# Two interleaved recurrent layers on one core: the last two segments projected in one pass, one-layer steps reordered, the down projection in column pairs, idle transposes ahead of the last block

## The chip, the cores and the metric

One core of one Trainium2 chip. The metric is device microseconds of one execution; the kernel before took 1579.52 us, the median of three runs (1578.43 to 1586.14).

## The reference

The program runs the same pair twice over 2048 tokens of width 448: a recurrent attention (A), then a gated feed-forward block (B), each behind a layer norm and with a residual.

```
x = x + A(layernorm(x));  x = x + B(layernorm(x))
x = x + A(layernorm(x));  x = x + B(layernorm(x))

A: mem = mem0                                  # 8 rows
   for each of 64 segments of 32 tokens:
       h = concat(mem, segment)                # 40 rows
       q, k, v = h Wq, h Wk, h Wv              # 16 heads of 256
       p = softmax(mask(q k^T / 16))           # causal; the memory rows see all rows
       o = (p v) Wo
       mem, out = o[:8], o[8:]
B: up = x W_up;  gate = x W_gate;  out = (relu(gate) * up) W_down     # width 1792
```

The memory rows make the segments of one layer follow one another. Inputs, weights and output are bfloat16.

## The kernel before, in words

**Setup.** Wq and Wk are fused into A_sb (and A3, A3z for the last 64 dimensions), Wv and Wo into B_sb, so that one segment needs: projection of h by A_sb (`prj`), scores with h itself (`Sm` for the 8 memory rows, `Sx` for the 32 segment rows), softmax (`weights_begin`, `weights_end`), weighting of h by the probabilities (`weigh_m`, `weigh_x`, tiles `ya`, `yb`, `ym`, `y1`, `y2`), and projection by B_sb (`project_out`, tile `ox`, 168 matmuls, and `project_tail`, tile `o3`, 56 matmuls in two column halves of the array for the last 64 dimensions).

**Steps.** The two layers run interleaved: step g works on segment g of the first layer (chain 0) and on segment g-4 of the second (chain 1, LAG = 4). So steps 0 to 3 have chain 0 alone, steps 4 to 63 both, steps 64 to 67 chain 1 alone. The output of a segment's tokens is projected one step later than its memory rows: step g weighs the tokens of its segment at the end (`weigh_x` writes YY[hf] of the next step) and step g+1 projects them together with its own memory rows. The columns that a projection reads run from `lo` to `hi`: 80 where both chains are there, 40 or 32 in one-layer steps. Step 68 has no chain and only projects the tokens of segment 67. YY holds Y0, Z0 (first half of the heads) and Y1, Z1 (second), taken in turn by the parity of the step.

**Feed.** Two segments of 32 make a block of 64 tokens. `Feed(i)` does for block i of the first layer (partitions 64 to 127 of its tiles) and block i-2 of the second (partitions 0 to 63) what follows attention: residual add (`residual`, which flips OT by TensorE, tile `otp`), layer norm (`norm`, and `row_stats` on DVE and POOL), the flip of tokens to columns (`xposed`: four transposes `tps`, then xT is copied by DVE and ACT), `gate_up` in seven parts (tiles `ups`, `gps`, 28 matmuls each, two row halves of the array), `down` (tile `dps`, 14 matmuls of 448 columns), the norm for the next layer (`norm2`), `feed_on` and `leave`, which writes the output. Odd steps from 3 on carry Feed((g-3)/2), cut into the step's matmuls; Feed(33) follows step 68. Feeds 0 and 1 have only a first-layer block, 32 and 33 only a second-layer block: there `self.n` is 64 of the 128 columns.

**Order.** TensorE's matmuls keep the written order (`in_order` chains them). DVE, ACT and POOL run their own queues in an order that a scheduler sets. PSUM tiles named "ps" come from one pool of seven banks, taken in turn.

In one-layer steps the written order behind the scores was: Sx of the first half, the Feed's flip of tokens, Sm and Sx of the second half, the flip of PM0 (`pps`), `weigh_m`, then `project_out`. POOL fills the tiles TZ0 and TZ1 with pieces of the identity before the first step (L405).

Of the kernel before, what the change touches and what calls it, by code (L numbers as in the profile page):

```python
# [8 lines left out]
BF = mybir.dt.bfloat16  # L9
# [44 lines left out]
def build_kernel(ctx, tc, A_x, A_mem0, A_Wq, A_Wk, A_Wv, A_Wo, B_W_gate, B_W_up, B_W_down, out,  # L54
# [29 lines left out]
    def tr(*a):  # L84
        in_order(nc.tensor.transpose(*a))  # L85
# [125 lines left out]
        nc.vector.tensor_copy(mem_cols(g, cs)[:, 0:n], src)  # L211


    with tc.tile_pool(name="pre", bufs=3) as pre:
        mem0_n = pre.tile([MEM, 512], BF, name="mem0_n", bufs=1)
        nc.gpsimd.dma_start(mem0_n[:, 0:DM], mem0)
# [110 lines left out]
            load_next()  # L327
            return transposed(nat[i], i == 0)

        warm = psum.tile([P, 2 * DM], BF, tag="ps", name="warm")  # L330
        def idle(n):
            for _ in range(n):
                tr(warm[:, 0:128], ident[:], ident[:])

        idle(32)
        cur = flip_next(0)
        idle(16)
# [70 lines left out]
    nc.vector.memset(OT[:], 0.0)  # L408
    xT = main.tile([P, NPASS, 128], BF, name="xT")
    hh = main.tile([P, FT, 128], BF, name="hh")  # L410
    nc.gpsimd.memset(hh[:], 0.0)
    HK = []
    for i in range(2):
# [5 lines left out]
    class Feed:  # L419


        def __init__(self, i):
            self.i = i
            self.first = i < nblk
            self.second = 0 <= i - LAG // BLK < nblk
            self.n = slice(0 if self.second else TB, P if self.first else TB)
            self.x = xa[i % 3]
            self.nx = xp[i % 2]

        def residual(self):  # L430
            tp = flipped_dims("otp", lambda r, kd: OT[ROWS[r], kd, :])
# [7 lines left out]

        def xposed(self):  # L440
            tps = transpose_tokens(self.xn)
            nc.vector.tensor_copy(xT[:, 0:4, :], tps[:])
            for r in range(2):
                nc.scalar.copy(xT[ROWS[r], 4:NPASS, :], tps[ROWS[1 - r], 0:3, :])  # L444

        def gate_up(self, u):
            n = self.n
# [12 lines left out]

        def down(self):
            i = self.i
            dps = self.dps = psum.tile([P, 512], F32, tag="ps", name="dps")
            for f in range(FT):
                mm(dps[:, 0:DM], hh[:, f, :], Wd_sb[:, f, :], start=(f == 0), stop=(f == FT - 1))
            if self.first:
                nc.vector.tensor_tensor(self.nx[TB:P, :], dps[TB:P, 0:DM], self.x[TB:P, :], op=ALU.add)
# [11 lines left out]
        def leave(self):  # L479
            i = self.i  # L480
            if self.second:
                nc.vector.tensor_tensor(self.x[0:TB, :], self.dps[0:TB, 0:DM], self.x[0:TB, :], op=ALU.add)
                nc.sync.dma_start(out_dram[block(i - LAG // BLK)], self.x[0:TB, :])

        def feed_on(self):
# [103 lines left out]
        nc.vector.tensor_copy(PT[:], pps[:].rearrange("p b q -> p (b q)"))  # L589
        return PT  # L590

    def flipped_rows(srcs):
# [7 lines left out]
        PT = main.tile([P, n * 128], BF, tag=f"PTr{n}", name="PT")  # L600
# [9 lines left out]
    def step(g, ff):  # L610
# [4 lines left out]
        hb = hTb[gb % 2]  # L615
        cols = [(0, 32) if c == 0 else (48, 80) for c in xs] + [(32, 40) if c == 0 else (40, 48) for c in ms]
        lo, hi = min(a for a, _ in cols), max(b for _, b in cols)
        ox = None

        def ys(hf, later=0):  # L620
# [62 lines left out]

        def weigh_x(hf, hk, PT):

            def keep(eng, c, t0, src):
                n = src.shape[-1] // SEG
                dst = ys(hf, 1)[:, t0:t0 + n, XO[c]:XO[c] + SEG]
# [12 lines left out]
            for kd in (2, 3):  # L701
                for c in chains:
                    rows = slice(64 * c, 64 * c + L)
                    mm(y2[c][:, kd * 256 - 512:kd * 256 - 256], hk[rows, kd, :], PT[rows, 0:256], start=True, stop=True)
            for c in chains:
                keep(nc.scalar if c == 0 else nc.vector, c, 16, y2[c][:, 0:256])
                tail = y2[c][:, 256:512].rearrange("p (o e i q) -> p e i o q", o=2, e=2, i=4)
                for e in range(2):
                    rows = slice(64 * e, 64 * e + 64)
                    evac(nc.vector if c == 0 else nc.scalar,  # L710
                         ys(hf, 1)[rows, 24:28, XO[c]:XO[c] + SEG].rearrange("p i (o q) -> p i o q", q=16),
                         tail[rows, e])

        def project_out(hf, t0, t1):

            nonlocal ox
            if ox is None:
                ox = psum.tile([P, 3, W], F32, tag="ox", bufs=1, name="ox")
            for t in range(t0, t1):
                for mc in range(3):  # L720
                    mm(ox[:, mc, lo:hi], B_sb[:, hf, t, mc * 128:(mc + 1) * 128],
                       ys(hf)[:, t, lo:hi], start=(hf == 0 and t == 0 and mc == 0),
                       stop=(hf == 1 and t == NT - 1 and mc == 2), skip_group_check=True)

        def project_tail():

            o3 = psum.tile([P, W], F32, tag="ps", name="o3")
            for hf in range(2):
                for t in range(0, NT, 2):
                    for e in range(2):  # L730
                        mm(o3[64 * e:64 * e + 64, lo:hi], B_sb[:, hf, t + e, 384:DM], ys(hf)[:, t + e, lo:hi],
                           start=(hf == 0 and t == 0), stop=(hf == 1 and t == NT - 2))
# [6 lines left out]
            for c in xs:  # L739
                x = slice(XO[c], XO[c] + SEG)  # L740
                nc.vector.tensor_tensor(ot_cols(c)[:, 3], o3[:, x], swap[:, x], op=ALU.add)

        def ot_cols(c):
            o = (g - 1) % BLK * SEG + (TB if c == 0 else 0)
# [2 lines left out]
        def finish():  # L747
            if ms:
                src = ox[:, :, M0:M0 + 16].rearrange("p k (c m) -> p k c m", m=MEM)
                set_mem(g + 1, src[:, :, ms[0]:ms[-1] + 1, :], ms, 3)  # L750
            for c in xs:
                nc.scalar.copy(ot_cols(c)[:, 0:3], ox[:, :, XO[c]:XO[c] + SEG])

        def feed(*us):
            if ff is not None:
# [34 lines left out]
        close_bank(c0, chains, hb, j, nc.scalar)  # L790
        close_bank(c2, chains, hb, j, nc.scalar)
        close_bank(c1, chains, hb, j, nc.vector)
        close_bank(c3, chains, hb, j, nc.scalar)
        if len(chains) == 2:
            pm = flipped(PM[0], 1, "m0")
            Sx0 = scores_x(0)
            weigh_m(0, hk, pm)
            if ff is not None:
                ff.xposed()
            scores_m(1)  # L800
            Sx1 = scores_x(1)
            probs_x(0, Sx0)
        else:
            Sx0 = scores_x(0)
            if ff is not None:
                ff.xposed()
# [122 lines left out]
```

## Time and profile before

| what | value |
|---|---|
| three runs | 1578.43, 1579.52, 1586.14 us |
| the profiled execution | 1585.95 us, span 1584.0 us |
| mean granted TensorE clock | 0.990 |
| PE busy | 1552.8 us, 98% of the span, 45116 matmuls |
| DVE, ACT, POOL busy | 1112.6, 783.1, 174.9 us |

A row of a group gives the line, the engine, the operation, what it writes and reads, its shape and count, then busy time in us, the mean duration of one in ns, and the engine's idle time just before, with what ended it. A row of the timeline starts with the start and the length in us; in brackets stands the idle time before it and its releaser. PEld is the loading of weights, which runs beside the matmuls; a matmul's duration holds a pipeline tail of some 0.16 us that the next one covers. "issue" means that the engine waited for nothing that the profile shows.

### The profile page before, as it was taken

Reading aid. Unit: us, or ns where it says so; the run is one execution under the profiler, and the core shown is the slowest. Engines: PE = TensorE matmul, PEld = TensorE weight load, DVE = VectorE, ACT = ScalarE, POOL = GpSimd, SP = SyncE. Lnnn points to the kernel's source line nnn. Section 1 sums busy time; section 2 is a strip of 40 time slices with the busy share of each in tenths; the row PEclk is TensorE's granted clock in tenths of the full one; section 3 lists DMA queues with packets and bytes.
Section 4 is the critical chain, followed back from the end, with each engine's and each line's share of the span. In section 5 each row is a group of like instructions: output and inputs, shape, how many; then the busy total and the mean of one; then the engine's idle time right before and its main releaser. Section 6 shows DMA issues by size and latency. Waiting matters only on the chain.

```text
span 1584.0 us, 98180 instructions
## 1 busy us (share of the span) xinstructions
PE 1552.8 (98%) x45116; PEld 1426.0 (90%) x45116; DVE 1112.6 (70%) x3825; ACT 783.1 (49%) x2307; POOL 174.9 (11%) x308
## 2 busy tenths in 40 slices
PE   9889999999999999999999999999999999999997
PEld 7588899999999999999999999999999999999885
DVE  6755677776777777776777677777767777777663
ACT  6634445544455545554455545544445545544442
POOL 3201110111011111111011111011001111011110
PEclk9989999999999999999999999999999999999998
DMA  9530000000000000000000000000000000000000
GB/s 284 148 80 8 9 10 5 9 10 10 10 10 10 10 10 6 8 10 10 10 10 10 10 10 7 7 10 10 10 10 10 10 10 8 6 8 7 7 7 6
DMA packets 29469, 33.13 MB, mean 21 GB/s; under 512 B 3320, under 2 KB 28160, under 8 KB 29056
## 3 DMA queue, kind: packets, MB, share of 16 engines
q1 hardware_dynamic: 28848, 26.74, 6.2%
q8 instruction: 353, 5.78, 1.5%
q14 instruction: 60, 0.49, 0.1%
q10 hardware_dynamic: 144, 0.11, 0.1%
q0 software_dynamic: 64, 0.01, 0.0%
HBM read 23.18 MB, written 1.84 MB: 16 GB/s over the span
## 4 chain that ended last, share of the span: by engine, by line
PE 95%; DVE 2%; issue 1%; ACT 1%; DMA 1%; POOL 1%; SPq 0%; POOLq 0%; ACTq 0%; DVEq 0%
PE prj L82 30%; PE ox L82 25%; PE ups L82 10%; PE dps L82 6%; PE o L82 5%; PE y L82 4%; PE Sx L82 3%; PE Sm L82 2%; PE aps L82 1%; PE pps L85 1%; PE gps L82 1%; PE bps L82 1%; PE tps L85 1%; PE kps L85 1%; PE ym L82 1%
## 5 line engine op out<-in xcount | busy, mean ns | idle before, releaser
L82 PEld LDWEIGHTS <-B_sb 128*128 128x128 bf16 (+1 forms) x15456 | 495.1, 103 | 29.6 <-issue 21.6
L82 PE MATMUL prj<-hT,A_sb 128*128 128x80 bf16 (+1 forms) x11424 | 430.7, 200 | 0.1
L82 PEld LDWEIGHTS <-A_sb 128*128 128x128 bf16 x11424 | 406.3, 100 | 8.5 <-issue 0.2
L82 PE MATMUL ox<-Y,B_sb 128*128 128x80 bf16 (+4 forms) x5880 | 223.1, 199 | 1.9 <-DVE Y L661 1.9
L94 ACT CAST TQ<-prj 128x480 bf16<-128x480 f32 (+1 forms) x380 | 183.1, 494 | 83.7 <-PE prj L82 59.2
L82 PE MATMUL ox<-Z,B_sb 128*128 128x80 bf16 (+2 forms) x5712 | 217.6, 199 | 1.3 <-DVE Z L661 1.3
L82 PE MATMUL ups<-xT,Wgu_sb 64*128 64x128 bf16 (+1 forms) x3332 | 191.3, 214 | 1.3 <-DVE hh L458 0.8
L82 PE MATMUL gps<-xT,Wgu_sb 64*128 64x128 bf16 (+1 forms) x3332 | 191.3, 214 | 0.4 <-ACT xT L444 0.3
L82 PEld LDWEIGHTS <-Wgu_sb 64*128 64x128 bf16 x6664 | 179.7, 95 | 4.4 <-issue 2.3
L96 DVE CAST TQ<-prj 128x480 bf16<-128x480 f32 (+1 forms) x228 | 129.5, 574 | 17.3 <-PE prj L82 11.7
L458 DVE SCALAR_TENSOR_TENSOR hh<-gps,ut 128x256 bf16<-128x256 f32 (+1 forms) x238 | 94.5, 407 | 48.2 <-ACT ut L457 35.4
L457 ACT CAST ut<-ups 128x256 bf16<-128x256 f32 (+1 forms) x238 | 85.5, 359 | 82.7 <-PE gps L82 64.1
L94 ACT CAST Y<-y 64x128 bf16<-64x128 f32 (+2 forms) x256 | 89.4, 379 | 46.5 <-DVE Y L96 41.5
L96 DVE CAST Y<-y 64x128 bf16<-64x128 f32 (+2 forms) x256 | 102.2, 420 | 14.2 <-ACT Y L94 4.3
L94 ACT COPY hT<-tps 128x256 bf16<-128x256 bf16 x32 | 11.9, 372 | 199.0 <-DVE hT L96 199.0
L96 DVE CAST Z<-y 64x128 bf16<-64x128 f32 (+2 forms) x256 | 99.2, 418 | 12.4 <-ACT Z L94 5.5
L589 DVE COPY PT<-pps 128x128 bf16<-128x128 bf16 (+1 forms) x206 | 49.9, 256 | 80.5 <-PE pps L85 77.7
L94 ACT CAST Z<-y 64x128 bf16<-64x128 f32 (+2 forms) x256 | 89.2, 378 | 23.8 <-DVE Z L96 17.4
L82 PE MATMUL dps<-Wd_sb,hh 128*128 128x448 bf16 x476 | 99.3, 362 | 0.0
L94 ACT CAST TZ<-prj 64x320 bf16<-64x320 f32 (+2 forms) x152 | 56.1, 380 | 86.4 <-DVE TZ L96 78.5
L577 DVE TENSOR_REDUCE ssum<-se 128x2 f32<-128x80 f32 (+1 forms) x270 | 70.8, 274 | 35.8 <-ACT se L571 33.6
L82 PE MATMUL prj<-hT,A 64*128 64x80 bf16 (+1 forms) x3264 | 93.9, 196 | 1.8 <-issue 1.4
(130 smaller groups left out, 2265.7 us busy)
## 6 DMA issues: line engine op xcount, KB each, us to landing
wo<-in_A_Wo_dram SPq DMA_DIRECT2D x8, 448.0 KB, 5.1
nat<-in_A_Wq_dram SPq DMA_DIRECT2D x8, 384.0 KB, 6.1
nat<-in_A_Wk_dram SPq DMA_DIRECT2D x8, 384.0 KB, 6.2
nat<-in_A_Wv_dram SPq DMA_DIRECT2D x8, 384.0 KB, 6.1
xa<-in_A_x_dram SPq DMA_DIRECT2D x32, 56.0 KB, 2.3
xa<-xp SPq DMA_DIRECT2D x32, 56.0 KB, 1.9
out_dram<-xa SPq DMA_DIRECT2D x32, 56.0 KB, 2.0
xp<-in_A_x_dram SPq DMA_DIRECT2D x30, 56.0 KB, 2.1
```

Of the source, the lines that this page charges most:

```text
L82: in_order(nc.tensor.matmul(*a, **k))
L85: in_order(nc.tensor.transpose(*a))
L94: nc.scalar.copy(dst, src)
L96: eng.tensor_copy(dst, src)
L457: nc.scalar.copy(ut[:, :, n], ups[:, :, n])
L458: nc.vector.scalar_tensor_tensor(out=hh[:, 2 * u:2 * u + 2, n], in0=gps[:, :, n], scalar=0.0, in1=ut[:, :, n], op0=ALU.max, op1=ALU.mult)
L577: nc.vector.tensor_reduce(ssum[:], se[:], axis=AX.X, op=ALU.add)
L589: nc.vector.tensor_copy(PT[:], pps[:].rearrange("p b q -> p (b q)"))
```

## The change

1. **Segments 66 and 67 of the second layer are projected together.** Step 66 writes the tokens' weighted rows 32 columns further left, step 67 writes its own beside them in the same tiles, projects nothing and ends behind `down` and `leave`; step 68 projects 64 columns at once and hands OT both segments.
2. **One-layer steps:** the flip of PM0 stands right behind Sx of the first half, and `weigh_m` before Sx of the second half. The Feed's flip of tokens stands between the last two projections; its norm runs on DVE in place of POOL.
3. **One-sided Feeds (0, 1, 32, 33):** `down` takes 64 columns of hh as weights and alternates between the two column halves of the array and two PSUM banks; `sum_up` adds the two parts and the residual (one ACT copy and two DVE adds in place of one DVE add). xT is copied for the 64 columns in use.
4. **Idle transposes:** 44 behind the last Feed's residual and 8 behind its flip, which is done twice so that DVE and ACT copy from tiles of their own. The helper `idle` is defined further up and takes a tile of 128 columns at each call.

```diff
+    def idle(n):
+        warm = psum.tile([P, 128], BF, tag="ps", name="warm")
+        for _ in range(n):
+            tr(warm[:], ident[:], ident[:])
...
         def xposed(self):
             tps = transpose_tokens(self.xn)
-            nc.vector.tensor_copy(xT[:, 0:4, :], tps[:])
+            nc.vector.tensor_copy(xT[:, 0:4, self.n], tps[:, :, self.n])
+            return tps
+
+        def xposed_rest(self, tps):
             for r in range(2):
-                nc.scalar.copy(xT[ROWS[r], 4:NPASS, :], tps[ROWS[1 - r], 0:3, :])
+                nc.scalar.copy(xT[ROWS[r], 4:NPASS, self.n], tps[ROWS[1 - r], 0:3, self.n])
...
         def down(self):
-            dps = self.dps = psum.tile([P, 512], F32, tag="ps", name="dps")
+            dps = self.dps = [psum.tile([P, 512], F32, tag="ps", name="dps") for _ in range(1 if self.both else 2)]
             for f in range(FT):
-                mm(dps[:, 0:DM], hh[:, f, :], Wd_sb[:, f, :], start=(f == 0), stop=(f == FT - 1))
+                if self.both:
+                    mm(dps[0][:, 0:DM], hh[:, f, :], Wd_sb[:, f, :], start=(f == 0), stop=(f == FT - 1))
+                else:
+                    mm(dps[f % 2][ROWS[f % 2], 0:DM], hh[:, f, self.n], Wd_sb[:, f, :], start=(f < 2), stop=(f >= FT - 2))
...
+        def sum_up(self, dst, o):
+            n = slice(o, o + TB)
+            if self.both:
+                nc.vector.tensor_tensor(dst[n, :], self.dps[0][n, 0:DM], self.x[n, :], op=ALU.add)
+                return
+            mine = o // TB
+            nc.scalar.copy(part[n, 1, :], self.dps[1 - mine][ROWS[1 - mine], 0:DM])
+            nc.vector.tensor_tensor(part[n, 0, :], self.dps[mine][n, 0:DM], self.x[n, :], op=ALU.add)
+            nc.vector.tensor_tensor(dst[n, :], part[n, 0, :], part[n, 1, :], op=ALU.add)
...
+        last = g == nseg + LAG - 1
+        now = 0 if chains else 1
+        if not chains:
+            lo -= SEG
...
+            kept = ys(hf, 0 if last else 1)
+            xo = (None, XO[1] - SEG) if g == nseg + LAG - 2 else XO
...
-            ff.norm(nc.gpsimd)
+            ff.norm(nc.gpsimd if len(chains) == 2 else None)
...
         close_bank(c1, chains, hb, j, nc.vector)
+        if ff is not None and len(chains) == 1:
+            tps = ff.xposed()
         close_bank(c3, chains, hb, j, nc.scalar)
+        if ff is not None and len(chains) == 1:
+            ff.xposed_rest(tps)
...
         else:
             Sx0 = scores_x(0)
-            if ff is not None:
-                ff.xposed()
+            pm = flipped(PM[0], 1, "m0") if ms else None
             scores_m(1)
+            weigh_m(0, hk, pm)
             Sx1 = scores_x(1)
-            pm = flipped(PM[0], 1, "m0")
-            weigh_m(0, hk, pm)
             probs_x(0, Sx0)
+        if last:
+            probs_x(1, Sx1)
+            feed(0, 1, 2, 3)
+            px0 = flipped_rows([(PX[0], 2)])
+            feed(4)
+            weigh_x(0, hk, px0)
+            feed(5)
+            px1 = flipped_rows([(PX[1], 2)], "x1")
+            feed(6)
+            weigh_x(1, hk, px1)
+            ff.down()
+            ff.leave()
+            return
...
     ff.residual()
+    idle(44)
     ff.norm()
     ff.xposed()
+    ff.xposed_rest(transpose_tokens(ff.xn))
+    idle(8)
     for u in range(FT // 2):
         ff.gate_up(u)
```

More of the change, by code (lines that the diff above doesn't have):

```diff
@@ L328, in flip_next @@
             return transposed(nat[i], i == 0)
[L330 to L333, printed above, removed]
         idle(32)
@@ L410, in build_kernel @@
     hh = main.tile([P, FT, 128], BF, name="hh")
+    part = main.tile([P, 2, DM], F32, name="part")
     nc.gpsimd.memset(hh[:], 0.0)
@@ L428, in __init__ @@
             self.nx = xp[i % 2]
+            self.both = self.first and self.second
         def residual(self):
@@ L481, in leave @@
             if self.second:
-                nc.vector.tensor_tensor(self.x[0:TB, :], self.dps[0:TB, 0:DM], self.x[0:TB, :], op=ALU.add)
+                self.sum_up(self.x, 0)
                 nc.sync.dma_start(out_dram[block(i - LAG // BLK)], self.x[0:TB, :])
@@ L599, in flipped_rows @@
                 tr(two[r][:, b, :], src[ROWS[r]], ident[ROWS[r], ROWS[r]])
-        PT = main.tile([P, n * 128], BF, tag=f"PTr{n}", name="PT")
+        PT = main.tile([P, n * 128], BF, tag=f"PTr{n}{tag}", name="PT")
         for r, eng in enumerate((nc.vector, nc.scalar)):
@@ L617, in step, with outs @@
         lo, hi = min(a for a, _ in cols), max(b for _, b in cols)
+        last = g == nseg + LAG - 1
+        now = 0 if chains else 1
+        if not chains:
+            lo -= SEG
+        def outs():
+            if not chains:
+                return [(slice(lo, lo + TB), OT[:, :, 0:TB])]
+            return [(slice(XO[c], XO[c] + SEG), ot_cols(c)) for c in xs]
         ox = None
@@ L721, in project_out @@
                     mm(ox[:, mc, lo:hi], B_sb[:, hf, t, mc * 128:(mc + 1) * 128],
-                       ys(hf)[:, t, lo:hi], start=(hf == 0 and t == 0 and mc == 0),
+                       ys(hf, now)[:, t, lo:hi], start=(hf == 0 and t == 0 and mc == 0),
                        stop=(hf == 1 and t == NT - 1 and mc == 2), skip_group_check=True)
@@ L730, in project_tail @@
                     for e in range(2):
-                        mm(o3[64 * e:64 * e + 64, lo:hi], B_sb[:, hf, t + e, 384:DM], ys(hf)[:, t + e, lo:hi],
+                        mm(o3[64 * e:64 * e + 64, lo:hi], B_sb[:, hf, t + e, 384:DM], ys(hf, now)[:, t + e, lo:hi],
                            start=(hf == 0 and t == 0), stop=(hf == 1 and t == NT - 2))
@@ L738, in project_tail @@
                                         swap[:, both].rearrange("p (c m) -> p c m", m=MEM), op=ALU.add)
-            for c in xs:
-                x = slice(XO[c], XO[c] + SEG)
-                nc.vector.tensor_tensor(ot_cols(c)[:, 3], o3[:, x], swap[:, x], op=ALU.add)
+            for x, ot in outs():
+                nc.vector.tensor_tensor(ot[:, 3], o3[:, x], swap[:, x], op=ALU.add)
         def ot_cols(c):
@@ L750, in finish @@
                 set_mem(g + 1, src[:, :, ms[0]:ms[-1] + 1, :], ms, 3)
-            for c in xs:
-                nc.scalar.copy(ot_cols(c)[:, 0:3], ox[:, :, XO[c]:XO[c] + SEG])
+            for x, ot in outs():
+                nc.scalar.copy(ot[:, 0:3], ox[:, :, x])
         def feed(*us):
@@ L798, in step @@
             if ff is not None:
-                ff.xposed()
+                ff.xposed_rest(ff.xposed())
             scores_m(1)
```

9 lines of the change are left out of this document (4 added, 5 removed).

## The prediction

> **What bounds the kernel now.** I read the page first: slices, engine shares, chain, costliest groups.
>
> ```profile
> PEclk9989999999999999999999999999999999999998
> PE 95%; DVE 2%; issue 1%; ACT 1%; DMA 1%; POOL 1%; SPq 0%; POOLq 0%; ACTq 0%; DVEq 0%
> L82 PEld LDWEIGHTS <-B_sb 128*128 128x128 bf16 (+1 forms) x15456 | 495.1, 103 | 29.6 <-issue 21.6
> ```
>
> TensorE carries 95% of the chain that ended last, and the clock (one digit for each fortieth of the span) is below full only in an early slice and in the last. The change leaves the order of every engine in the two-layer steps 6 to 63 alone, so some 1,300 us of the span should stay as they are. What it touches are the one-layer steps 0 to 3 and 64 to 67, step 5's Feed, the drain (step 68) and the last Feed. So the windows of the end come next; columns: stretch, its length, then busy time of PE, PEld, DVE, ACT, POOL with counts, granted clock, DMA share, GB/s.
>
> ```profile
> 1549.50:1552.91 3.41, 2.20 (x71) 1.59 (x64) 1.53 (x5) 1.15 (x6) 0.00 (x0) 1.00 0.02 5
> 1552.91:1556.33 3.42, 3.42 (x12) 1.37 (x10) 0.17 (x1) 0.00 (x0) 0.00 (x0) 0.50 0.00 0
> ...
> 1566.57:1569.98 3.41, 0.91 (x33) 0.69 (x29) 1.26 (x4) 0.24 (x1) 0.63 (x2) 1.00 0.00 0
> 1569.98:1573.39 3.41, 1.95 (x46) 1.64 (x48) 1.03 (x3) 1.08 (x3) 0.17 (x1) 0.50 0.00 0
> 1573.39:1576.81 3.42, 3.42 (x138) 3.42 (x133) 1.44 (x5) 1.19 (x5) 0.00 (x0) 0.50 0.02 5
> ```
>
> A thinly filled stretch of 3.41 us at clock 1.00 (PE busy 2.20, then 0.91) is followed each time by one or more at 0.50. Idle TensorE is thus paid twice, and the last Feed runs mostly at half clock. Then the timeline and the groups by form of steps 67, 68 and the last Feed:
>
> ```profile
> 1543.14 0.23 PE L82 MATMUL Sx<-maskS,ident 128*128 128x160 bf16 x1
> 1551.46 0.97 PE L82 MATMUL o<-Z,B_sb 128*64 128x32 bf16 x50 [1.21 <-issue]
> L82 PE MATMUL dps<-Wd_sb,hh 128*128 128x448 bf16 x14 | 4.5, 503 | 0.0
> L82 PE MATMUL ox<-Y,B_sb 128*128 128x32 bf16 x168 | 4.6, 185 | 0.0
> 1567.52 0.29 PE L85 MATMUL otp<-ident,OT 64*128 64x64 bf16 x8 [0.33 <-ACT OT L752]
> 1570.64 0.61 PE L85 MATMUL tps<-ident,xn 128*128 128x128 bf16 x4 [2.83 <-DVE xn L187]
> 1571.74 0.97 ACT L444 COPY xT<-tps 64x384 bf16<-64x384 bf16 x2 [4.28 <-DVE xT L442]
> L82 PE MATMUL ups<-xT,Wgu_sb 64*128 64x64 bf16 x98 | 5.3, 230 | 0.5 <-DVE xT L442 0.5
> 1580.15 0.62 DVE L482 TENSOR_TENSOR xa<-dps,xa 64x448 bf16<-64x448 f32 x1 [2.18 <-PE dps L82]
> ```
>
> Sx0 of step 67 starts at 1543.14, the drain's output is flipped at 1567.52, 24.4 us later; the last matmul ends near 1580.15 and one DVE add and the output's DMA follow. All of this is serial. The sum below goes part by part over this profiled execution: 1585.95 us, of which 1584.0 are the span and 1.95 lie around it.
>
> **Steps 67 and 68 as one projection.** Removed from step 67: 168 ox and 56 o matmuls, the swap copies and adds behind them, and a flip whose result nobody read. Step 68 does the same counts once, 64 columns wide. What 64 columns cost is not in the trace; it lies between these:
>
> ```profile
> L82 PE MATMUL ox<-Y,B_sb 128*128 128x80 bf16 x84 | 3.3, 202 | 0.0
> 182.24 1.20 PE L82 MATMUL o<-Z,B_sb 128*64 128x80 bf16 x56
> L82 PE MATMUL ups<-xT,Wgu_sb 64*128 64x64 bf16 x56 | 1.8, 190 | 0.0
> L82 PE MATMUL y<-PT,hk 40*128 40x256 bf16 x4 | 0.6, 272 | 0.0
> ```
>
> At 32 columns an ox takes 4.6/168 = 27 ns, at 80 columns 3.3/84 = 39 ns at most (the group's busy time holds other matmuls' gaps). Estimates for 64: 27 to 35, taken 29, since the 80-column time is mostly columns and scales to 31, less the tail; 168 x 29 = 4.9 us. The o pairs take 1.2 less the tail, 1.0 us, at 80 columns, so no more at 64.
>
> Step 67 itself becomes softmax, gate_up 0 to 6 and the two weighings interleaved, then down. Is that bound by PE or by DVE? PE: 196 gate_up matmuls (half of them ups, half gps beside them) at 1.8/112 = 16 ns, 3.0 us with the tail off; twice the 0.6 of the y row, 1.1 without tails; flips 0.2 (estimate); down 1.35 (next part): 5.6 us behind the scores, which end at about 1544.3 (estimate: Sx0 and Sx1 of 0.25 each and the wait for TQ1's last copy between them). DVE by the same stretch now:
>
> ```profile
> L458 DVE SCALAR_TENSOR_TENSOR hh<-gps,ut 128x128 bf16<-128x128 f32 x7 | 2.0, 287 | 0.6 <-ACT ut L457 0.2
> L96 DVE CAST Y<-y 128x512 bf16<-128x512 f32 (+1 forms) x2 | 1.0, 547 | 0.0
> L582 DVE TENSOR_TENSOR PX<-se,rs 128x160 bf16<-128x160 f32 x2 | 0.6, 320 | 0.0
> L570 DVE TENSOR_TENSOR se<-Sx,mx 128x160 f32<-128x160 f32 x2 | 0.6, 318 | 0.0
> L568 DVE TENSOR_REDUCE mx<-Sx 128x4 f32<-128x160 f32 x2 | 0.6, 318 | 0.2 <-PE Sx L82 0.2
> L577 DVE TENSOR_REDUCE ssum<-se 128x4 f32<-128x160 f32 x2 | 0.6, 304 | 0.4 <-ACT se L571 0.4
> ```
>
> Softmax 2.4 and 0.3 of reciprocals (estimate), hh 2.0, Y now needed twice 2.0, two PT copies 0.5 (estimate): 7.2 us, from 1543.8 on. The last hh stands ahead of the second Y, so about 6.2 us of it and 0.6 of idle lie before the end of down: down ends near 1552.0 (PE-bound 1550, with waits at every flip 1553.5). The evacuation of Y for the second half (1.0 us) hides under down and the first o matmuls. Then 1.0 + 4.9 + 0.35 for the OT copy: otp at 1558.3 against 1567.52, **9.2 us** less (7.7 to 11). Part of this is the half clock of the first windows: the 14 dps took 4.5 us there.
>
> **Down in column pairs**, for the four one-sided Feeds. At full clock and at half:
>
> ```profile
> 183.37 2.82 PE L82 MATMUL dps<-Wd_sb,hh 128*128 128x448 bf16 x14
> L82 PE MATMUL dps<-Wd_sb,hh 128*128 128x448 bf16 x14 | 4.4, 494 | 0.0
> ```
>
> (step 5, step 3). 2.82 less the tail is 2.66, 190 ns each. That two 64-column tiles run side by side is shown by o: 56 in 1.0 us, 18 ns each at 80 columns, half of ox. So 7 x 190 = 1.33. Step 5: **1.3**. Step 3: 4.4 falls to 1.33 if its window stays at full clock, 2.7 if not; the added second DVE add (0.5, estimate from the 0.62 row) lengthens nx, statistics, norm2 ahead of the tps in project_out, and I charge 0.3 for that new wait: **2.6** (1.0 to 2.9). Behind the ACT copy of dps on its queue wait only evacuations with slack. Step 67 is counted above.
>
> **Flip and weighting moved.** Step 0 first:
>
> ```profile
> 79.66 0.10 PEld L82 LDWEIGHTS <-TZ 128*128 128x128 bf16 x1 [2.21 <-POOL TZ L405]
> 81.66 0.48 PE L82 MATMUL ox<-Y,B_sb 128*128 128x8 bf16 x13 [0.47 <-DVE Y L661]
> ```
>
> Sx1 waits for POOL's fill of TZ1 to 79.66 and, after a second wait, ends at 80.3; flip, ya, yb and their evacuation come only then. Moved ahead, they hide in that wait; ox starts at 80.3: **1.3**. The half clock that follows this hole may end a window sooner: **0.4** (0 to 0.8). Steps 1, 2, 64 and 66, by step 1:
>
> ```profile
> 97.52 0.24 DVE L582 TENSOR_TENSOR PM<-se,rs 128x80 bf16<-128x80 f32 x1
> 98.73 0.21 DVE L589 COPY PT<-pps 128x128 bf16<-128x128 bf16 x1
> 99.44 0.41 DVE L661 CAST Z<-ya 128x256 bf16<-128x256 f32 x1
> 99.91 0.26 PE L82 MATMUL ox<-Z,B_sb 128*128 128x40 bf16 x4 [0.53 <-DVE Z L661]
> ```
>
> PM is done at 97.76, so the flip can stand right behind Sx0; the copy PT moves from 98.73 to about 98.2, Y's copy to about 99.0, ox to 99.45: 0.47 earlier. But DVE's softmax of the second mem half is now behind it, and the next flip, 69 ox later, would wait some 0.2. **0.3** each, 1.2 together (-0.5 to 2). In steps 3 and 65 the earlier tps eats the same amount: 0. Their norm moves from POOL to DVE, hidden under the projections.
>
> **The last Feed.** The chain otp, DVE adds, statistics, POOL, xn is the same 3.1 us (1567.52 to 1570.64). The 44 idle transposes fill it. Were they slower than the 2.83 us wait, they would delay tps:
>
> ```profile
> 8.47 1.82 PE L85 MATMUL warm<-ident 128*128 128x128 bf16 x16
> 10.13 0.49 PE L82 MATMUL aps<-two 128*128 128x384 bf16 x2
> 10.45 0.22 PE L82 MATMUL mxw<-two 128*128 128x64 bf16 x2
> ```
>
> 16 took 1.66 us (8.47 to 10.13) at the cold start, 104 ns each; half that at full clock, 44 x 52 = 2.3 us: hidden. Do they hold the clock? Ahead of 10.13 stand nothing but transposes, and the first 384-column aps follow at 160 ns each (10.13 to 10.45), half of what a half clock gives. So transposes count. The Trainium skill, "TensorE: Matmul & The Clock Gate", section "Part 4: PE-mode transpose", says the opposite: the full clock does not engage for transpose mode. By that rule gate_up would stay at the 5.3 us of its row and the idle transposes could take 44 x 104 = 4.6 us; this row of the trace speaks against it.
>
> At full clock: tps, and the two xT copies (0.97, half as wide now and from a tile of their own) cost 1.25 us up to where gate_up can run on, then 2.6, down 1.33: 5.2 us from xn instead of 9.5. Less 0.55 for the second add at the end. The waits named "issue" are the open price: after each narrow gate_up TensorE stood 1.2 us with no releaser (1551.46 above). I charge 1.0: 4.3 - 0.55 - 1.0 = **2.7** (1.3 to 3.7).
>
> **Sum.** 9.2 + 1.3 + 2.6 + 1.3 + 0.4 + 1.2 + 2.7 = 18.7 us: 1585.95 becomes 1567.3. The three timed runs have a median of 1579.52, 6.4 below the profiled execution; the same 18.7 off gives **1561**. All high ends together: 22 us, 1557; all low ends: 12 us, 1567.
>
> **Rivals.** (1) Transposes do not count, and the idle ones run at half clock: the last Feed loses about 1.8 on the way to tps and 2.5 in gate_up, the sum falls to 14.8: 1565. Against it the cold start. Chance 0.08. (The rule of the Trainium skill's page "TensorE: Matmul & The Clock Gate" above comes to this.) (2) Column pairs do not overlap, so the change doesn't do what it says: 1.33 lost four times, 13.4 left: 1566. Against it the o rows. 0.06. (3) Step 67 becomes a chain score, exp, flip, weigh with PE waiting at each link, and two further waits of 1.3 on issue: 3 to 5 lost, 1565. 0.12. (4) Slower: the instruction stream is cut in another place in every step after the first, and waits on issue fall on the path. Now they are 21.6 us before B_sb loads (page row) and mostly covered. If each of the 58 unchanged two-layer steps uncovered 0.4, that is 23 us, 1584; it decides from 0.32 a step on. Against it: such waits already meet all positions of the steps and hardly reach the chain (issue 1%). 0.03.
>
> **How the numbers follow.** Forecast 0.71, rivals 0.08, 0.06, 0.12, 0.03. Range 1555 to 1569: the bounds 1557 to 1567 widened for the spread of the three runs (1578.43 to 1586.14). What a measurement here can tell from no change is about 0.5%, 8 us: faster means under 1571.6, which the forecast and rivals 1 to 3 all reach unless two of them meet: 0.92; same 0.05; slower 0.03.
>
> **Right or wrong.** The profile after should show otp about 15 us behind step 67's Sx0, 14 dps in 1.35 us in four places, clock 1.00 from step 67 to the last matmul, no wait for POOL's TZ longer than before with ox right behind it, and equal times for steps 6 to 63. Wrong would be: a clock of 0.50 in the last gate_up, PE waits on issue or PX adding over 4 us in step 67, or a middle that moved by microseconds.

## The result and the profile after

The changed kernel takes 1568.88 us, the median of six runs (1566.24 to 1572.97); the kernel before, in six runs, 1581.68 us (1578.43 to 1586.84). The ratio is 0.9917, with a 95% interval of 0.9895 to 0.9938: 12.8 us less, where 18.7 were forecast. The prediction's time was 1561, its range 1555 to 1569. The profiled execution of the changed kernel took 1572.97 us with a span of 1571.2, at a mean clock of 0.992.

The page first: the clock by fortieths of the span, the chain of work that ended last, and the costliest group.

```profile
PEclk9989999999999999999999999999999999999999
PE 94%; DVE 3%; ACT 1%; POOL 1%; issue 1%; DMA 1%; SPq 0%; POOLq 0%; ACTq 0%; DVEq 0%
L82 PEld LDWEIGHTS <-B_sb 128*128 128x128 bf16 (+1 forms) x15232 | 489.8, 103 | 25.9 <-issue 18.7
```

The last slice no longer shows an 8, TensorE still carries 94% of the chain, and there are 224 fewer B_sb loads: the 168 and 56 of one projection. The digits hide one stretch, which the windows of the end show (columns: stretch, length, busy PE, PEld, DVE, ACT, POOL with counts, granted clock, DMA share, GB/s):

```profile
1544.64:1548.06 3.42, 2.23 (x94) 1.93 (x89) 2.02 (x9) 1.81 (x8) 0.00 (x0) 1.00 0.02 5
1548.06:1551.47 3.41, 3.41 (x22) 1.61 (x22) 1.31 (x3) 0.52 (x2) 0.00 (x0) 0.50 0.00 0
...
1558.30:1561.71 3.41, 3.15 (x56) 2.94 (x54) 2.02 (x7) 0.02 (x1) 0.79 (x2) 1.00 0.02 5
1561.71:1565.12 3.41, 3.41 (x206) 3.21 (x202) 1.54 (x7) 2.21 (x8) 0.00 (x0) 1.00 0.02 5
```

Step 67 has lost a window: its interleaved stretch keeps PE busy for only 2.23 of 3.42 us, and the next window, which holds `down`, runs at 0.50. In the last Feed the clock is 1.00 in both windows where it was 0.50 before. TensorE's timeline of step 67 and the last Feed:

```profile
1538.10 0.29 PE L85 MATMUL kps<-ident,hT 64*128 64x64 bf16 x8
...
1540.72 0.23 PE L82 MATMUL Sx<-maskS,ident 128*128 128x160 bf16 x1
...
1547.91 0.90 PE L82 MATMUL y<-PT,hk 40*128 40x256 bf16 x4 [0.62 <-ACT PT L94]
...
1552.39 5.07 PE L82 MATMUL ox<-Z,B_sb 128*128 128x64 bf16 x168
1557.88 0.29 PE L85 MATMUL otp<-ident,OT 64*128 64x64 bf16 x8 [0.41 <-ACT OT L781]
1558.10 2.63 PE L85 MATMUL warm<-ident 128*128 128x128 bf16 x44
1560.99 0.66 PE L85 MATMUL tps<-ident,xn 128*128 128x128 bf16 x8 [0.26 <-DVE xn L187]
```

The groups by form: `down` of step 67 and gate_up of the last Feed.

```profile
L82 PE MATMUL dps<-Wd_sb,hh 128*64 128x448 bf16 x14 | 2.8, 581 | 0.0
...
L82 PE MATMUL gps<-xT,Wgu_sb 64*128 64x64 bf16 x98 | 3.1, 190 | 0.0
```

From Sx0 to otp it is 17.16 us (forecast: about 15; 24.4 before). Here `down` takes 2.8 us, at half clock. gate_up of the last Feed takes 3.1 us in place of 5.3, with no wait on issue.

To place the difference I compare stages, from the first `kps` flip of one step to that of the next (us; "again" is a second profiled execution of the same code, from the experiments below):

| stage | before | before again | changed | changed again | forecast gain |
|---|---|---|---|---|---|
| start to step 0 | 73.34 | 73.63 | 76.40 | 74.02 | 0 |
| 0 | 21.31 | 21.48 | 19.92 | 19.59 | 1.7 |
| 1 | 15.31 | 15.42 | 15.39 | 15.94 | 0.3 |
| 2 | 16.57 | 15.76 | 16.13 | 17.84 | 0.3 |
| 3 | 26.75 | 23.95 | 23.79 | 24.06 | 2.6 |
| 5 | 26.25 | 25.72 | 24.42 | 24.12 | 1.3 |
| 9 to 59 | 1137.90 | 1137.86 | 1138.29 | 1137.90 | 0 |
| 64 | 17.08 | 17.11 | 16.54 | 16.54 | 0.3 |
| 65 | 23.83 | 23.66 | 24.56 | 24.56 | 0 |
| 66 | 15.28 | 15.37 | 15.41 | 15.13 | 0.3 |
| 67 to otp | 26.71 | 24.48 | 19.78 | 18.27 | 9.2 |
| otp to the last DVE add's end | 13.25 | 13.23 | 10.12 | 10.12 | 2.7 |

### The profile page after: what moved, and what is told of

Read it like the earlier page. It is cut to its first block, busy times and chain, and to the rows that moved or that the text cites. A ratio compares the mean times of both kernels' runs of the same rounds, so it can differ in the third digit from the quotient of the medians.

```text
span 1571.2 us, 97832 instructions
## 1 busy us (share of the span) xinstructions
PE 1544.7 (98%) x44947; PEld 1420.5 (90%) x44947; DVE 1115.5 (71%) x3833; ACT 783.8 (50%) x2309; POOL 168.1 (11%) x302
## 4 chain that ended last, share of the span: by engine, by line
PE 94%; DVE 3%; ACT 1%; POOL 1%; issue 1%; DMA 1%; SPq 0%; POOLq 0%; ACTq 0%; DVEq 0%
PE prj L82 29%; PE ox L82 24%; PE ups L82 10%; PE dps L82 6%; PE o L82 5%; PE y L82 4%; PE Sx L82 3%; PE Sm L82 2%; PE aps L82 1%; PE bps L82 1%; PE pps L85 1%; PE gps L82 1%; PE tps L85 1%; PE kps L85 1%; PE ym L82 1%
## 5 line engine op out<-in xcount | busy, mean ns | idle before, releaser
L82 PEld LDWEIGHTS <-B_sb 128*128 128x128 bf16 (+1 forms) x15232 | 489.8, 103 | 25.9 <-issue 18.7
L82 PE MATMUL ox<-Y,B_sb 128*128 128x80 bf16 (+3 forms) x5712 | 218.5, 199 | 0.6 <-DVE Y L688 0.6
L94 ACT CAST Y<-y 128x512 bf16<-128x512 f32 (+1 forms) x252 | 88.3, 380 | 43.5 <-DVE Y L96 39.8
L96 DVE CAST Y<-y 128x512 bf16<-128x512 f32 (+1 forms) x252 | 100.1, 418 | 12.1 <-ACT Y L94 4.3
L589 ACT ACTIVATE se<-se 128x80 f32<-128x80 f32 (+1 forms) x270 | 71.4, 298 | 50.4 <-DVE se L588 43.6
```

The costliest lines, as they stand in the source:

```text
L82: in_order(nc.tensor.matmul(*a, **k))
L94: nc.scalar.copy(dst, src)
L96: eng.tensor_copy(dst, src)
L589: nc.scalar.activation(se[:], se[:], AF.Exp, scale=SCALE)
```

## The experiments

**The kernel before, once more** (the old code within the new file; no diff to the kernel before).

> The kernel before, profiled a second time, for its setup alone. In the two profiles so far the first step's flip of hT (kps of step 0) starts at 73.34 us before and at 76.40 us after; TensorE stood 0.83 and 2.34 us on issue at the same place of the setup. Theory S (scatter of instruction loading beside the full weight transfer): this run's kps of step 0 falls anywhere between 73 and 77 us. Rival C (the change lengthens the setup, by the idle helper's tile or by where the instruction stream is cut): this run is at 73.3 +- 0.3 again, and all kernels that hold the changed helper are at 76 to 77. From step 1 to the end both expect the times of the first profile within 1.5 us.

Measured: 1580.16 us, beside 1581.79 of the kernel before. From step 67's kps to otp it takes 24.48 us, not 26.71. TensorE's timeline of this run, step 3 and then step 67:

```profile
137.64 0.91 PE L82 MATMUL o<-Z,B_sb 128*64 128x40 bf16 x46 [0.47 <-issue]
138.48 2.82 PE L82 MATMUL dps<-Wd_sb,hh 128*128 128x448 bf16 x14
...
1537.16 0.29 PE L85 MATMUL kps<-ident,hT 64*128 64x64 bf16 x8
...
1547.28 0.97 PE L82 MATMUL o<-Z,B_sb 128*64 128x32 bf16 x50 [0.93 <-issue]
1548.17 2.82 PE L82 MATMUL dps<-Wd_sb,hh 128*128 128x448 bf16 x14
...
1561.64 0.29 PE L85 MATMUL otp<-ident,OT 64*128 64x64 bf16 x8 [0.33 <-ACT OT L752]
```

And the same two places in the profile of before that the prediction rests on:

```profile
139.04 0.92 PE L82 MATMUL o<-Z,B_sb 128*64 128x40 bf16 x46 [1.41 <-issue]
139.90 4.44 PE L82 MATMUL dps<-Wd_sb,hh 128*128 128x448 bf16 x14
...
1552.37 4.51 PE L82 MATMUL dps<-Wd_sb,hh 128*128 128x448 bf16 x14
```

The same code runs both `down` at full clock here and at half clock there, and stands 0.47 and 0.93 us on issue here, 1.41 and 1.21 there. Together (4.44 - 2.82) + (1.41 - 0.47) + (4.51 - 2.82) + (1.21 - 0.93) = 4.5 us of the 5.9 by which the two profiled executions differ (1580.77 and 1574.88 to the last add). That is scatter of one code. All but the 0.94 of the issue wait in step 3, so 3.6 us, had gone into the prediction's terms as gain. The executions behind the median have no profile of their own; that they hold less of this scatter is read from their times alone. The expectation that the two profiles agree within 1.5 us behind the setup was wrong: from step 0 to the last add it is 1507.43 us in the first and 1501.25 in this one. The setup, 73.63 us, fits both theories.

**No idle transposes.**

```diff
-    idle(44)
...
-    idle(8)
```

> The changed kernel without the 44 and the 8 idle transposes of the last Feed. Theory A (transposes count as activity and hold the clock): the clock falls to 0.50 in or ahead of the last gate_up; gate_up takes 5.0 to 5.5 us in place of 3.07, dps up to 2.7 in place of 1.52, and from otp to the last DVE add it takes 12 to 13.5 us in place of 10.1. Rival R (transposes do not count; the changed kernel kept its clock for another reason, the wider ox ahead of it): clock 1.00 and 10.1 us +- 0.3 without them too.

Measured: 1568.79 us. The first of the last Feed's two windows at half clock:

```profile
1553.94:1557.35 3.41, 2.86 (x72) 2.56 (x74) 1.16 (x4) 0.90 (x3) 0.00 (x0) 0.50 0.02 5
```

TensorE's timeline of this run, and then its gate_up group by form:

```profile
1536.10 0.23 PE L82 MATMUL Sx<-maskS,ident 128*128 128x160 bf16 x1
...
1543.44 1.51 PE L82 MATMUL dps<-Wd_sb,hh 128*64 128x448 bf16 x14
...
1551.25 0.29 PE L85 MATMUL otp<-ident,OT 64*128 64x64 bf16 x8 [0.41 <-ACT OT L781]
1554.37 1.03 PE L85 MATMUL tps<-ident,xn 128*128 128x128 bf16 x8 [2.82 <-DVE xn L187]
```

```profile
L82 PE MATMUL gps<-xT,Wgu_sb 64*128 64x64 bf16 x98 | 5.5, 236 | 0.1
```

Without the transposes the two windows of gate_up (this one and the next) fall to 0.50 and it takes 5.5 us, as before the change; otp to `down` takes 9.68 us instead of 7.23. So the idle transposes hold the clock and are worth 2.45 us, as theory A had it. From otp to the last add it takes 10.1 us in all seven profiles that have the transposes, the merging and `down` in pairs (11.1 in the one without merging, which has a wait on issue of 0.84). Without the transposes it takes 12.6 here and some 13.2 in both profiles of before. The Trainium skill, "TensorE: Matmul & The Clock Gate", section "Part 4: PE-mode transpose", says that the full clock does not engage for transposes; these two traces say otherwise, with 1.00 behind them and 0.50 without them. The run's total is no longer than the changed kernel's all the same, since its step 67 met no half clock: Sx0 to otp is 15.15 us and `down` 1.51, as forecast.

**Idle transposes in step 67 too**, 4 + 4 + 12 at its thin places.

```diff
             feed(0, 1, 2, 3)
+            idle(4)
             px0 = flipped_rows([(PX[0], 2)])
+            idle(4)
             feed(4)
...
             feed(6)
+            idle(12)
             weigh_x(1, hk, px1)
             ff.down()
```

> The changed kernel with 20 more idle transposes in step 67: 4 ahead of the first flip of PX, 4 behind it, 12 ahead of the second weighing, where TensorE waits now (0.62 and 0.36 us and several shorter ones). Theory T (the half clock from 1548.06 to 1551.47 came of a thinly filled window, and cost step 67's down 1.2 us): clock 1.00 up to the end, the 14 dps 1.45 us in place of 2.61, step 67's Sx0 to otp 16.0 us in place of 17.16. Rival P (the pairs of this down do not overlap, whatever the clock): dps 2.6 us again. Rival D (the idle transposes stand in the way, since the waits are shorter than they): down at full clock, but Sx0 to otp 17 us or more.

Measured: 1567.08 us. The window over the end of the interleaved stretch and the start of `down`:

```profile
1541.90:1545.31 3.41, 3.04 (x61) 2.13 (x57) 2.39 (x7) 1.40 (x6) 0.00 (x0) 1.00 0.02 5
```

The window is filled to 3.04 us and the clock stays at 1.00. From kps to otp it takes 18.63 us, 1.15 less than the changed kernel's profiled execution. `down` takes 1.51 us, as theory T had it. But the unfilled step 67 takes 18.03 to 18.84 in five other profiles (19.26 in the one with `down` in one chain), none of them with a half clock there: it came in one profile of seven. Filling insures against some 1.3 us that are seldom lost. A cost of the filling can't be told from scatter: Sx0 to otp is 15.74 us here, and 15.15, 15.38 and 16.07 in three profiles with the unfilled code of step 67. In the total nothing of it shows.

**Down in one chain of 128 columns.**

```diff
-                if self.both:
+                if True:
```

(in `down` and `sum_up`, with one dps tile.)

> The changed kernel with down and its sum as before in all Feeds (one bank, 14 matmuls of 128 columns of weights, one DVE add). Forecast's pricing: dps 2.66 us in place of 1.45 at steps 3, 5 and in the last Feed at full clock, and 2.7 to 5.2 in step 67; the last Feed's end 0.7 shorter by the second add: steps 3 and 5 longer by 1.2 each, otp to the last DVE add 10.1 + 1.2 - 0.7 = 10.6 us. Rival: the second add and the ACT copy cost as much as the pairs save, so step 3 to 4 is within 0.4 us of the changed kernel's 23.8 us, as tps of feed_on waited 0.35 us for xn there.

Measured: 1570.80 us. TensorE's timeline, `down` of step 5 in this run, and then in the changed kernel `down` of step 5 and of the last Feed:

```profile
178.17 2.82 PE L82 MATMUL dps<-Wd_sb,hh 128*128 128x448 bf16 x14
```

```profile
181.10 1.52 PE L82 MATMUL dps<-Wd_sb,hh 128*64 128x448 bf16 x14
...
1565.11 1.51 PE L82 MATMUL dps<-Wd_sb,hh 128*64 128x448 bf16 x14
```

1.30 us less in each, and in step 3 (1.52) as well. What arrives, close to the forecast's pricing except in step 3: 1.2 in step 5 (25.63 against 24.42), 0.87 in step 3 (24.66 against 23.79), 0.6 in the last Feed, where the second add takes 0.72 back (last matmul to the last add's end 0.65 and 1.37).

**No merging of the two segments** (step 67 projects segment 66 again, step 68 segment 67; down in pairs kept).

```diff
-        last = g == nseg + LAG - 1
-        now = 0 if chains else 1
-        if not chains:
-            lo -= SEG
+        last, now = False, 0
...
-            xo = (None, XO[1] - SEG) if g == nseg + LAG - 2 else XO
+            xo = XO
```

> The changed kernel with segments 66 and 67 projected one after the other again (step 67 projects, step 68 has 32 columns); all other parts stay. Forecast's term: step 67's kps to otp is 9.2 us longer than the changed kernel's (19.8, 18.0 at full clock), that is 27 to 29 us. Rival H (the forecast read a kernel that had lost clock there; at full clock the merge saves what 168 ox and 56 o matmuls cost, 4.2 + 1.0, and the two waits between step 67 and 68): 23 to 24.5 us, 5 to 6 longer than the 18.0.

Measured: 1574.52 us beside 1581.57 of before. TensorE's timeline from step 67 to the drain:

```profile
1534.45 0.29 PE L85 MATMUL kps<-ident,hT 64*128 64x64 bf16 x8
...
1542.15 0.19 PE L82 MATMUL gps<-xT,Wgu_sb 64*128 64x64 bf16 x1 [0.86 <-issue]
...
1545.62 0.81 PE L82 MATMUL o<-Z,B_sb 128*64 128x32 bf16 x41 [0.92 <-issue]
...
1558.41 0.29 PE L85 MATMUL otp<-ident,OT 64*128 64x64 bf16 x8 [0.33 <-ACT OT L776]
```

From kps to otp 23.96 us, with the clock at 1.00 all the way. The merged forms without a half clock take 18.0 to 18.8: merging alone is worth 5 to 6 us, and two waits on issue (1.8 us) go with it. That is rival H, and not the forecast's 27 to 29 us.

**Flip and weighting back behind Sx of the second half.**

```diff
-            pm = flipped(PM[0], 1, "m0") if ms else None
             scores_m(1)
-            weigh_m(0, hk, pm)
             Sx1 = scores_x(1)
+            pm = flipped(PM[0], 1, "m0") if ms else None
+            weigh_m(0, hk, pm)
```

> The changed kernel with the old order in one-layer steps (Sm and Sx of the second half, then the flip of PM0 and its weighting); the Feed's early flip of tokens stays. Forecast: step 0 to 1 (kps to kps) 21.3 us in place of 19.9, steps 1, 2, 64 and 66 each 0.3 longer, steps 3 and 65 equal. Rival N (outside step 0 the move gives nothing: what ya no longer waits for, the next flip or Sm waits for): step 0 to 1 21.3, all others within 0.15 of the changed kernel.

Measured: 1574.46 us. Step 0 takes 21.30 us (19.92 in the changed kernel), step 64 17.07 (16.54), steps 1 and 2 15.25 and 15.50 (15.39 and 16.13): step 0's gain is 1.4, step 64's 0.5, and in steps 1 and 2 nothing is seen. Step 66 takes 15.58 us (15.41 and 15.13 in the changed kernel's two profiles). Step 65, expected equal, takes 26.60 us in place of 24.56: its first ox stands 6.56 us behind kps instead of 5.67, its window there has TensorE busy for only 1.93 of 3.41 us, and the next one, from 1504.91 on, runs at 0.50. So in step 65 the move is worth 0.9 us and, in this execution, a half clock; step 3 shows nothing of the kind (23.47 us here, 23.79 in the changed kernel). TensorE's timeline of step 0 in this run, where the weighting follows the wait for POOL's TZ and ox starts 2.0 us behind its end, and then in the changed kernel, where ox starts 0.6 us behind it:

```profile
82.92 0.19 PE L82 MATMUL Sx<-hT,TZ 128*128 128x40 bf16 x1 [2.10 <-POOL TZ L405]
...
84.92 1.98 PE L82 MATMUL ox<-Y,B_sb 128*128 128x8 bf16 x69 [0.47 <-DVE Y L688]
```

```profile
82.74 0.19 PE L82 MATMUL Sx<-hT,TZ 128*128 128x40 bf16 x1 [1.18 <-POOL TZ L405]
...
83.35 1.96 PE L82 MATMUL ox<-Y,B_sb 128*128 128x8 bf16 x69
```

**Step 65: three ways to be rid of its new wait.** Step 65 became 0.7 to 0.9 us slower in the changed kernel, which was not forecast. The changed kernel's timeline of TensorE, and then of DVE:

```profile
1498.13 0.29 PE L85 MATMUL kps<-ident,hT 64*128 64x64 bf16 x8
...
1499.56 0.27 PE L82 MATMUL Sm<-hT,TQ 128*128 128x80 bf16 x3 [0.51 <-DVE TQ L96]
...
1503.80 0.91 PE L82 MATMUL ox<-Z,B_sb 128*128 128x40 bf16 x30 [0.21 <-DVE Z L688]
```

```profile
1498.64 0.61 DVE L187 TENSOR_SCALAR xn<-xa,mv,rstd 128x448 bf16<-128x448 bf16 x2 [0.73 <-POOL rstd L178]
1499.16 0.35 DVE L96 CAST TQ<-prj 128x192 bf16<-128x192 f32 x1
```

DVE now makes xn, and the copy TQ that the first scores need stands behind it. Norm back on POOL:

```diff
-            ff.norm(nc.gpsimd if len(chains) == 2 else None)
+            ff.norm(nc.gpsimd)
```

> The changed kernel with the Feed's norm on POOL in one-layer steps, as before; the early flip of tokens stays. Theory Q (Sm of steps 3 and 65 waits 0.48 us because DVE's TQ copy is queued behind xn): that wait is gone here. But POOL takes 2.46 us for xn where DVE takes 0.6, so the early tps should now wait, 0.5 to 1.2 us, and step 65 to 66 is 24.5 to 25.3 us in place of 24.55. Rival (Sm waits for its matmuls, not for DVE's queue): the 0.48 stays.

Or that copy on ACT:

```diff
-        close_bank(b1, chains, hb, j, nc.vector)
+        close_bank(b1, chains, hb, j, nc.scalar if ff is not None and len(chains) == 1 else nc.vector)
```

> The changed kernel with the TQ copy of bank b1 moved from DVE to ACT in the three one-layer steps that carry a Feed. Theory Q: the 0.48 us wait at Sm of steps 3 and 65 goes, step 65 to 66 is 24.1 us in place of 24.55, step 3 to 4 23.4 in place of 23.8. Rival (another wait follows at once: ya's for PT or ox's for Y, or ACT becomes late with the copies of c0 and c2): step 65 to 66 within 0.15 of 24.55.

Or the old order whole in steps 3 and 65 (norm on POOL, flip of tokens behind Sx0, weighting behind Sx1), with 15 idle transposes in step 67:

```diff
-            ff.norm(nc.gpsimd if len(chains) == 2 else None)
+            ff.norm(None if last else nc.gpsimd)
...
-        if ff is not None and len(chains) == 1:
+        if last:
             tps = ff.xposed()
...
+            if ff is not None and not last:
+                ff.xposed_rest(ff.xposed())
+                scores_m(1)
+                Sx1 = scores_x(1)
+                pm = flipped(PM[0], 1, "m0")
+                weigh_m(0, hk, pm)
+            else:
...
+            idle(5)
...
+            idle(10)
```

> The changed kernel with steps 3 and 65 in the old order whole (norm on POOL, flip of tokens behind Sx of the first half, flip of PM0 and its weighting last), step 67 and the steps without a Feed in the new one, and 5 and 10 idle transposes in step 67 behind the first flip of PX and ahead of the second weighing. Theory E (the early flip of tokens is what made step 65 slower by 0.7 to 0.9 us, as neither the norm on POOL nor TQ's copy on ACT alone brought it back): step 65 to 66 23.7 us, step 3 to 4 22.8 (the old 23.95 less 1.2 for the pairs), step 67's kps to otp 18.1 at clock 1.00, total 2 us under the changed kernel's, ratio to before about 0.988. Rival W (another wait sets these steps, the order does not matter): 24.4 and 23.7 again.

Run beside it on the same chip, the changed kernel once more:

> The changed kernel once more, beside the one above and with five rounds, for its undisturbed size. From the stages measured so far (setup 73 to 77 us whatever the kernel; from step 0 to the end 1489 to 1492 us changed, 1501 to 1507 before): 10 to 15 us less than before, ratio 0.990 to 0.9935. If the setup were longer through the change, its kps of step 0 would be at 76 us again; by scatter it is nearer to 73.

Measured: norm on POOL 1566.93 us and step 65 24.42; the copy on ACT 1567.21 and 24.30; the old order in those steps 1568.06 (median of five) and 23.79, what the kernel before takes (23.83 and 23.66). TensorE's timeline of step 65 in the three runs, in this order:

```profile
1495.33 0.34 PE L85 MATMUL tps<-ident,xn 128*128 128x128 bf16 x3 [0.25 <-POOL xn L187]
...
1495.91 0.23 PE L85 MATMUL tps<-ident,xn 128*128 128x128 bf16 x1 [0.24 <-POOL xn L187]
```

```profile
1497.39 0.23 PE L85 MATMUL pps<-ident,PM 128*128 128x128 bf16 x1 [0.38 <-DVE PM L600]
...
1498.35 0.27 PE L82 MATMUL ya<-PT,hk 128*128 128x128 bf16 x2 [0.59 <-DVE PT L607]
```

```profile
1497.18 0.29 PE L85 MATMUL kps<-ident,hT 64*128 64x64 bf16 x8
...
1502.25 0.91 PE L82 MATMUL ox<-Z,B_sb 128*128 128x40 bf16 x30 [0.40 <-DVE Z L688]
```

From kps to the first ox of 30 it is 5.67 us in the changed kernel and 5.07 with the old order (5.10 before: 1501.70 to 1506.80). With the norm on POOL the wait moves to the early flip itself, which POOL feeds no sooner; with the copy on ACT it moves to PM and PT on DVE, and 24.30 us lies between theory Q's 24.1 and its rival's 24.4. So moving one step to another engine does not bring the time back. That the place of the flip, ahead of the scores, is what costs is the reading that is left. It is not shown by itself: the old order puts back norm, flip and weighting together, and no run has the late flip with the early weighting. Step 3 did not follow: with the old order it took 23.60 us against 23.79, where 22.8 were expected, and step 67 took 18.67 us from kps to otp, where 18.1 were.

In all, the old order in these two steps has a ratio of 0.9911 (0.9892 to 0.9929) and the changed kernel beside it, 1567.95 us, 0.9916 (0.9899 to 0.9932), both to the kernel before at 1581.36: the 0.8 us of step 65 can't be told apart in the total, where 2 us were expected, and no faster version is claimed.

## Why the prediction was right, and where its sum was off

The forecast (faster, within the range) holds, but 1568.88 us lies 0.12 under the range's upper end of 1569; that it falls inside owes something to luck. The mechanism holds for the merging, the column pairs, step 0 and the idle transposes, each by an experiment of its own; the narrower xT copies had none, and the gains expected in steps 1, 2 and 66 and most of that in step 3 did not come. Of its signs: otp 15.38 us behind Sx0 came in the changed kernel's second profile and 15.15 in the run without idle transposes, 17.16 in the first profile; the clock was 1.00 from step 67 to the end but for one window; `down` took 1.52 us (1.35 and a tail) in three places and 2.8 in step 67; TZ's wait was shorter and ox right behind it; steps 9 to 59 moved by 0.4 us at most. No rival came true: transposes hold the clock (the run without them shows it, while the cold start alone was thin evidence, read from durations: the profile's rows grant 1.00 there, even where 16 transposes took 104 ns each), column pairs overlap, the waits of step 67 add up to 1.8 us (0.6 on the ACT copy of PT, 0.4 each on TQ and Z, 0.2 each on hh and issue) and, without a half clock, it still is 15.15 from Sx0 to otp, and nothing happened in the unchanged middle.

The time was 7.9 us too low. 2.2 of it is the median of before, 1579.52 in three runs and 1581.68 in six. The rest is the sum, 18.7 against 12.8, and the step of it that failed is "the same 18.7 off": a sum made against one profiled execution was taken off a median 6.4 us below it, although the terms for steps 3 and 67 held half-clock `down` of that execution as the kernel's own cost. The repeat of the kernel before shows 1.62 + 1.69 + 0.28 = 3.6 of them to be scatter, which leaves 15.1. Of the other 2.3, step 65 is 0.8, step 3 some 1 and steps 1, 2 and 66 are 0.9, less 0.4 that the last Feed gave beyond its forecast. The merging fell a further 0.5 to 1.3 short and step 5 gave up to 0.8 more, so the parts close to about 1 us and no better. Two sums in the prediction have slips that change no time by more than 1 us: its high ends add up to 23.0, not 22, and rival 1's losses of 1.8 and 2.5 leave 14.4, not 14.8. By terms:

- **Merging, 9.2:** 6.9 between the profiles, 5.6 to 6.5 between undisturbed runs (24.48 to 18.0 and 18.8; 5 to 6 for the merging alone). The 64-column ox, taken at 29 ns, took 5.07/168 = 30 ns, and Sx0 to otp came as forecast in the profiles named above (15.15 and 15.38). But the sum left Sx0 where it was, 2.33 us behind kps; with the Feed's flip of tokens now ahead of it, it stands at 2.62 to 2.89. From kps to otp the new side, forecast at 17.5, took 18.0 to 18.8. The old side was 1.7 + 0.3 too dear. In the changed kernel's own profile a half clock in `down` gave back 1.3 (2.8 against 1.51).
- **Step 3, 2.6:** 0.2 and -0.1 between the repeat of before (23.95) and the two profiles of the changed kernel. `down` fell by 1.30 as forecast, but it starts 0.6 later behind kps (12.82 us against 12.19 in the repeat), and behind it the step takes 0.5 longer, 0.35 of that in the wait for xn behind the second add, where 0.3 were charged. The first ox is late by the same 0.6 (5.93 against 5.33); with the old order it is at 5.92 all the same, so the cause in this step stays open. "Hidden under the projections" was wrong for the norm on DVE: the TQ copy is queued behind it, and Sm waits 0.51 for that.
- **Step 65, 0:** 0.7 to 0.9 lost, 0.57 of it ahead of the first ox. The wait for TQ is part of it, though taking that away gave back only 0.26 (24.56 to 24.30). The prediction asked who waits for the ACT copy of dps, and not who waits behind xn on DVE.
- **Step 5, 1.3:** 1.3 to 2.1 by the table, 1.2 by undoing it. **Step 0, 1.3 and 0.4:** 1.4 to 1.9 by the table, 1.4 by undoing it; that the half clock ended sooner is not seen as a term of its own.
- **Steps 1, 2, 64, 66, 0.3 each:** 0.5 in step 64, nothing that can be told from scatter in the others (step 2 took 15.3 to 17.8 us in the profiles of the changed kernel and its variants; the longest has 1.88 us on issue and a half clock behind it). That the expected wait at the next flip ate the gain is argued, not tested.
- **Last Feed, 2.7:** 3.1. The charge of 1.0 for issue did not come in this profile (0.84 did in the run without merging), and the second add cost 0.72, not 0.55.
- **Setup, 0:** 3.06 longer between the profiles. The same code took 74.02 in its second profile, and the kernels that share it 72.48 to 77.02, so this is scatter too. In the changed kernel's first profile its main place is one wait; in the profile of before that wait is 0.83 us:

```profile
45.78 0.32 PE L85 MATMUL tpw<-ident,nat 64*128 64x64 bf16 x9 [2.34 <-issue]
```

Its window has TensorE busy for 1.07 of 3.41 us, and the next one runs at 0.50. In the two other long setups (76.6 and 77.0 us) the half clock stands elsewhere, at about 60 us. What sets these waits is open.

## What to carry to other kernels

Before a gain is computed against one profiled execution, take a second one of the same code: terms that rest on a half-clock window or a wait on issue may be that execution's alone, and they don't come off the median. Where a TensorE wait of about 3 us stands ahead of dense work, harmless transposes in it pay (2.45 us here); in step 67, where the thin stretch held 2.2 to 2.5 us of work in 3.4, they gained nothing that shows in the total. When a step moves to another engine, list what is queued behind it there, not only what runs beside it.

## What the runs showed of the hardware

In these traces the half clock comes in whole windows of 3.41 us, mostly behind a thinly filled one. Whether a thin stretch of code makes a thin window depends on where the grid of windows falls: step 67's interleaved stretch gave 2.23 us in the window that begins 6.5 us behind kps, and then 0.50, while in the run without idle transposes, whose windows these are, the window begins 7.1 us behind kps and has 2.54, and then 1.00:

```profile
1540.28:1543.70 3.42, 2.54 (x85) 2.01 (x79) 2.42 (x8) 1.56 (x7) 0.00 (x0) 1.00 0.03 5
1543.70:1547.11 3.41, 3.41 (x116) 2.91 (x113) 2.10 (x5) 1.47 (x5) 0.00 (x0) 1.00 0.02 5
```

The Trainium skill, "TensorE: Matmul & The Clock Gate", section "Part 1: The HAM clock gate (the "warmup" mystery)", says that the activity window is free-running, so that one kernel meets it in another phase each time; the traces agree, with 0.50 in step 67's `down` in one profile of the changed kernel and in step 2 in the other.

Busy time alone does not decide. In both profiles of before, the window ahead of step 68's projection is busy for 3.13 and 3.15 us, mostly with matmuls of 32 columns, and the next one is at half clock all the same; here are the two of the first profile:

```profile
1559.74:1563.15 3.41, 3.13 (x110) 2.66 (x106) 1.02 (x2) 1.11 (x5) 0.00 (x0) 1.00 0.03 5
1563.15:1566.57 3.42, 3.42 (x135) 3.42 (x132) 0.19 (x1) 0.00 (x0) 0.00 (x0) 0.50 0.02 5
```

And behind step 0's first ox, which have 8 columns, four windows in a row of that profile are filled (3.41 us each) and run at 0.50. How busy time and width go together is not worked out here.

What a half-clock window costs differs by what runs in it: `down` with 448 columns went from 190 to 310 ns a matmul on the mean (2.66 to 4.35 us for 14, tails off, 3.41 of them at half clock), while from the first of step 68's 168 ox of 32 columns to otp it took 4.91 us in the repeat of before, with the clock at 0.50 from 1557.25 to 1560.66, and 4.71 at full clock in the run without merging. In this pair the narrow matmuls are a cheap place for a half clock to fall.
